# Selecting each expert's top 80 tokens by ranks instead of by MAX8 rounds, in a sparse attention and expert kernel

## The chip, the cores and the metric

The kernel runs on one NeuronCore of a Trainium2 chip. The metric is the device time of one execution in microseconds (us). Five engines work side by side: TensorE (PE, with its weight loads shown apart as PEld), VectorE (DVE), ScalarE (ACT), GpSimd (POOL) and SyncE (SP, which here only issues DMAs). They meet only through semaphores.

## The reference, cut to what matters

```
# attention: B=4 batches, H=8 heads, S=768 tokens, D=64; keys in chunks of 32
ub     = sum(max(q*kmin, q*kmax))          # bound of each chunk's score
top    = 6 chunks of the largest ub, causal
attn   = softmax(scale * q@k.T, masked to those chunks and to earlier keys)
x      = (attn @ v), as rows (B*S, H*D) = (3072, 512)
# experts: E=8, capacity 80
logits = x @ w_gate ; expert = argmax ; gate = max of softmax(logits)
for e in range(E):
    tok = tokens of expert e ; if more than 80: the 80 with the largest gate
    out[tok] = gate[tok] * (relu(x[tok] @ w1[e]) @ w2[e])      # all other rows 0
```

## The kernel before, in words

The attention loop has 16 steps `i`, one for each pair of heads; four pairs make a batch (`b = i // 4`, pair 0 to 3 of it). In a step, `scores` (L489) computes six blocks of transposed scores on TensorE, half of each in turn in the PSUM tiles SC0 and SC1, and ScalarE takes the exponentials into EXB (key E0 to E5). `folds` (L514) masks the diagonal blocks on GpSimd and adds the blocks up into ES, from which `sums` (L545) on TensorE makes the softmax denominators. `values` (L531) multiplies by v into OB, ScalarE copies that to oT. The sums, the row transposes (`rows`, L562) and the scaling of pair `i - 1` stand inside the step of pair `i`, so that GpSimd has a step's time for its additions. `bounds`, `transposes`, `unselT` prepare later pairs. `scale_rows` (L567) writes the rows `x` to DRAM (x_rows) by a DMA of SyncE, and the pair's share of the logits to lgp.

The order on every engine is the order in which this code is written: the helper `op` (L72) puts each instruction at the end of its engine's queue and adds the semaphore waits for the tiles it reads and writes.

When a batch has all its pairs, the next batch's pair 0 makes its gates: `gate_in` and `gate` (VectorE: row maxima, argmax, gate value), `gate_digits` (VectorE: the token's number and its gate in three bf16 parts, per expert, in RC), and `gate_T` (L603: six transposes into SC0 and one ScalarE copy to `cand`, 8 rows, one for each expert). Then `rounds` spreads ten rounds over the batch's pairs: MAX8 finds the eight largest of a row of 848 (768 new tokens and the 80 kept), MATCH_REPLACE8 takes them out.

After the loop comes the tail. The last pair's sums, rows, scaling and the last batch's gate run one behind the other; ten more rounds on rows of 768 (L724), a merge with the 80 kept ones, the threshold of each expert (L729), masks, two matmuls and a scan that number the chosen tokens (L738 to L753), one-hot rows (L759) and 24 matmuls (L764) give `idx`, the 80 token numbers of each expert. Eight indirect DMAs of GpSimd gather these rows (L781), and eight experts run: `turn`, `up`, `down` and an indirect DMA of the result (L821). The experts' weights come by DMAs of GpSimd's queue during the loop (`wload`, two or one in a step); w2 of the last expert takes the place of E0 and E1 in EXB after the loop. Eight memsets on GpSimd in the tail (L723) clear the gathers' destinations. `warm` issues matmuls whose result nobody reads; 40 of them stand ahead of the first pair.

## Time and profile before

| | us |
|---|---|
| median of 3 runs | 349.25 (348.21 to 350.11) |
| the profiled execution: its own time | 347.47 |
| its span, first to last instruction | 345.7 |
| busy in the span: PE, PEld, DVE, ACT, POOL | 288.7, 183.4, 232.9, 149.3, 231.2 |

The span leaves out 1.77 us around the instructions. Busy times are of one execution and overlap; what they say of the end depends on who waits for whom, which the chain of waits and the timelines show. A PE record counts twice for an f32 matmul: eight f32 matmuls show as x16.

### The profile page before, as it was taken

The numbers are of one execution on the slowest core, as the hardware profiler recorded it, in microseconds if no ns is written. First come the engines' busy times: TensorE is split into PE (matmuls) and PEld (weight loads), VectorE is DVE, ScalarE is ACT, GpSimd is POOL, SyncE is SP. The second block draws the span as 40 slices with busy tenths as digits, with TensorE's granted clock in tenths as the row PEclk, the third lists the DMA queues.
The fourth block names the chain that finished last, engine by engine and source line by source line (L and its number), as shares of the span: only waits on it lengthen the run. The fifth ranks groups of instructions, "written<-read, shape, count | busy, mean of one in ns | idle before, by whom it ended". The sixth has DMA issues, their size and how long they took to land.

```text
span 345.7 us, 7895 instructions
## 1 busy us (share of the span) xinstructions
PE 288.7 (83%) x3244; PEld 183.4 (53%) x3244; DVE 232.9 (67%) x591; ACT 149.3 (43%) x202; POOL 231.2 (67%) x313
## 2 busy tenths in 40 slices
PE   7499999999989999998999999899999210126993
PEld 6356656575646566565656565656556100025771
DVE  3815435262988797979697887979797489871441
ACT  3265645555554646555555546554545000002320
POOL 5059888787868797786878787869798900007322
PEclk9789999999999999999999999999999955556999
DMA  9946879899758999798999779864907450001121
GB/s 175 193 91 139 150 145 184 240 225 165 160 101 184 266 196 189 151 161 258 183 179 191 140 151 255 144 108 87 163 11 138 58 86 1 0 2 55 53 59 57
DMA packets 104964, 47.50 MB, mean 137 GB/s; under 512 B 88955, under 2 KB 97269, under 8 KB 104928
## 3 DMA queue, kind: packets, MB, share of 16 engines
q1 hardware_dynamic: 89920, 27.94, 34.6%
q0 software_dynamic: 13440, 18.67, 33.1%
q10 hardware_dynamic: 1568, 0.39, 0.6%
q8 instruction: 25, 0.41, 0.5%
q14 instruction: 11, 0.09, 0.1%
HBM read 53.10 MB, written 10.75 MB: 185 GB/s over the span
## 4 chain that ended last, share of the span: by engine, by line
PE 73%; issue 12%; ACT 6%; POOL 4%; DVE 3%; DMA 1%; POOLq 0%; DVEq 0%
PE SC L498 23%; PE OB L539 20%; PE SC L425 6%; PE SC L504 5%; ACT EXB L509 5%; PE OB L815 4%; PE OB L564 3%; PE M L554 3%; PE SC L800 3%; PE M L549 2%; POOL ES L528 2%; PE MB L485 2%; DMA kn<-x_rows,idx 1%; ACT cand L607 1%; ACT unsT L487 1%
## 5 line engine op out<-in xcount | busy, mean ns | idle before, releaser
L528 POOL TENSOR_TENSOR ES<-ES,EXB 128x256 f32<-128x256 f32 (+1 forms) x112 | 106.1, 960 | 6.4
L509 ACT ACTIVATE EXB<-SC 128x1024 f32<-128x1024 f32 x96 | 86.3, 917 | 52.1 <-PE SC L504 50.4
L498 PE MATMUL SC<-qT,kT 64*128 64x512 f32 (+3 forms) x512 | 98.7, 473 | 2.8 <-ACT cand L607 2.7
L539 PE MATMUL OB<-EXB,vn 128*64 128x256 f32 (+2 forms) x704 | 71.9, 360 | 0.0
L539 PEld LDWEIGHTS OB<-EXB,vn 128*64 128x64 f32 x704 | 46.7, 137 | 23.0 <-issue 8.8
L498 PEld LDWEIGHTS SC<-qT,kT 64*128 64x128 f32 x512 | 42.4, 189 | 26.5 <-issue 15.5
L528 POOL TENSOR_TENSOR ES<-EXB 128x768 f32<-128x768 f32 (+1 forms) x32 | 49.3, 1542 | 1.3
L626 DVE MAX8 top<-cand 8x8 f32<-8x848 f32 (+1 forms) x40 | 40.3, 1008 | 2.2 <-ACT cand L607 1.3
L519 POOL TENSOR_SCALAR_AFFINE_SELECT EXB<-EXB 128x256 f32<-128x256 f32 x80 | 31.6, 406 | 12.1 <-ACT EXB L509 12.1
L504 PE MATMUL SC<-unsT,ind 64*128 64x384 bf16 (+3 forms) x256 | 39.0, 298 | 0.0
L543 ACT ACTIVATE oT<-OB 128x512 f32<-128x512 f32 (+1 forms) x32 | 15.7, 491 | 52.7 <-PE OB L539 52.7
L628 DVE MATCH_REPLACE8 cand<-top,cand 8x848 f32<-8x848 f32 (+1 forms) x36 | 35.7, 992 | 0.0
L572 DVE TENSOR_TENSOR xp<-OB,rden 128x768 bf16<-128x768 f32 x16 | 15.3, 958 | 24.4 <-PE OB L564 24.3
L781 POOL DMA_INDIRECT qn<-x_rows,idx x4 | 3.9, 980 | 35.0 <-issue 35.0
L504 PEld LDWEIGHTS SC<-unsT,ind 64*128 64x128 bf16 x256 | 13.0, 95 | 18.6 <-issue 8.5
L557 DVE STREAM_TRANSPOSE M<-M 128x192 f32<-128x192 f32 x16 | 6.2, 384 | 24.3 <-PE M L554 24.3
L467 DVE STREAM_TRANSPOSE M<-M 128x160 f32<-128x160 f32 x16 | 5.8, 366 | 21.5 <-PE MB L463 21.1
L430 ACT ACTIVATE qT<-SC 128x768 f32<-128x768 f32 x16 | 13.0, 812 | 14.7 <-PE SC L425 14.7
L792 ACT ACTIVATE rq<-MB 128x320 bf16<-128x320 bf16 x4 | 1.7, 437 | 39.3 <-PE MB L789 39.3
L519 POOL TENSOR_SCALAR_AFFINE_SELECT ES<-EXB 128x256 f32<-128x256 f32 x16 | 6.5, 404 | 17.6 <-PE M L554 16.3
L732 PE MATMUL M<-dg,ones 8*128 8x8 f32 x2 | 0.6, 367 | 20.9 <-DVE dg L730 20.9
L821 POOL DMA_INDIRECT out_dram<-EXB,idx x8 | 7.4, 920 | 14.6 <-DVE EXB L819 14.6
(141 smaller groups left out, 449.3 us busy)
## 6 DMA issues: line engine op xcount, KB each, us to landing
w1s<-in_moe_w_dram POOLq DMA_DIRECT2D x8, 1024.0 KB, 8.4
w2s<-in_moe_w_dram POOLq DMA_DIRECT2D x7, 1024.0 KB, 10.2
qn<-in_q_dram SPq DMA_DIRECT2D x32, 192.0 KB, 4.0
vn<-in_v_dram SPq DMA_DIRECT2D x32, 192.0 KB, 2.9
out_dram<-w1s SPq DMA_DIRECT2D x4, 1536.0 KB, 7.6
kn<-in_k_dram SPq DMA_DIRECT2D x30, 192.0 KB, 3.7
x_rows<-xp SPq DMA_DIRECT2D x16, 192.0 KB, 4.5
EXB<-in_moe_w_dram POOLq DMA_DIRECT2D x1, 1024.0 KB, 9.7
```

The costliest lines, as they stand in the source:

```text
L425: op("pe", lambda: pe.transpose(SC[ps][:, ts(t)], a, ident_f[:]), r=[f"{nm}{s}0", f"{nm}{s}1", "ident_f"], w=[f"SC{ps}"], inc=(t == NT - 1))
L498: op("pe", lambda: pe.matmul(o, kT[j][pr, ts(kt)], qT[j][pr, q0:q1], start=True, stop=False), r=[f"kT{j}", f"qT{j}"], w=[f"SC{s}"], inc=False)
L504: op("pe", lambda: pe.matmul(o, ind[pr, ts(kt)], unsT[j][pr, b0 - 128:q1 - 128], start=False, stop=True), r=[f"ind{h}", f"unsT{j}"], w=[f" ...
L509: op("act", lambda: ac.activation(Ex(st, None, 0, W), src, ACTF.Exp, scale=SCALE), r=[f"SC{s}"], w=[f"E{st}"])
L519: op("gp", lambda: gp.affine_select(ad, a, pattern=[[0, 2], [1, 128]], compare_op=ALU.is_ge, fill=0.0, base=0, channel_multiplier=-1), r=[ ...
L528: op("gp", lambda: gp.tensor_tensor(o, in0, in1, ALU.add), r=[f"E{s2}", f"E{first[0]}"] if first else [f"E{s2}"] + kt, w=kt)
L539: op("pe", lambda: pe.matmul(OB[pr, q0:q1], vn[s][:, kt, h, :], ex, start=(n == 0), stop=last), r=[f"vn{s}{h}", "ES0" if st is None else f ...
L543: op("act", lambda: ac.activation(oT[:, q0:q1], OB[:, q0:q1], ACTF.Copy), r=[f"O{bk}"], w=[f"oT{bk}"])
L572: op("dve", lambda: ve.tensor_tensor(xo, xi, rx, ALU.mult), r=["O0", "O1", "rden"], w=["xp"])
L626: op("dve", lambda: ve.max(dst, cv), r=["cand"], w=[f"top{int(last)}{n}"])
L628: op("dve", lambda: ve.match_replace(cv, dst, cv, -2.0), r=["cand", f"top{int(last)}{n}"], w=["cand"])
L815: op("pe", lambda: pe.matmul(o, hTv(e)[:, fb * CAP:(fb + 1) * CAP], w2v(e)[:, fb, :], start=(fb == 0), stop=(fb == FB - 1)), r=[f"hT{s}{fb ...
```

## The change

The rounds go, and the ranks of the tokens are counted. `rank_row` transposes the six columns of gates, each spread over 128 columns, and ScalarE copies the result to G: every partition holds the 768 gates of the batch in its row, and `rank_pred` puts a copy, a hair smaller, beside it (it settles ties by position). `rank_cmp` compares, for one tile of 128 tokens, 640 of the row's gates with the tile's own gate on each partition; `rank_own` and `rank_diag` do the same for the 128 tokens of the tile itself. `rank_count` multiplies these 0/1 tiles by the tokens' one-hot expert rows on TensorE (44 matmuls with 32 columns of weights): each token gets its rank among those of its expert. `rank_slot` turns ranks into one-hot rows of 80 slots, `table` multiplies them by RC, and `merge` takes, slot by slot, the larger of the 80 kept and of the 80 new in opposite order. `sort_rows`, `sort_rank` and `sort_apply` bring the 80 kept back into order after the second and third batch. For the batches 0 to 2 this is spread over pairs 0, 1 and 2 of the next batch; for the last one it is in the tail. The compare results of batches 0 to 2 lie in the weight tiles of the last two experts, whose loads move to the steps 14 and later.

The last pair's folds of block 5 are left out; `sums_last` sums their pieces with 72 matmuls instead. The pair's logits are scaled ahead of its rows. `clear_xg` clears the gathers' destinations on VectorE in steps 14 and 15. Three groups of dummy matmuls (56, 16, 44) stand in the tail.

```diff
                         if lo:
-                            folds(st)
+                            folds(i, st)
...
-                        for (s2, c2, q0, q1) in ADDS[st]:
+                        for (s2, c2, q0, q1) in ADDS[st] if st < 5 or i < NP - 1 else []:
...
+                def sums_last(i):
+                    pieces = [(None, 0, 0, 512), (2, 256, 512, 768)] + ADDS[5]
+                    for n, (st, c0, q0, q1) in enumerate(pieces):
+                        for h in range(2):
+                            for c in range(4):
...
+                                op("pe", lambda: pe.matmul(M0[c * 32:c * 32 + 32, q0 // 4:q1 // 4], onc[:, h, :], a,
+                                                           start=(n == 0 and h == 0), stop=False),
...
+                    sums_lg(i, False, True)
+                    sums_out()
...
-                def gate_T(b):
-                    for t in range(NT):
-                        op("pe", lambda: pe.transpose(SC[0][0:E, ts(t)], gv[:, b * NT + t, :], ident_f[:]),
...
-                    op("act", lambda: ac.activation(cand[:, CAP:CAP + S], SC[0][0:E, 0:S], ACTF.Copy), r=["SC0"], w=["cand"])
...
-                def top_round(n, last):
...
+                PRED = 1.0 - 2.0 ** -24
+
+                def rank_row(b):
+                    for t in range(NT):
+                        gb = bass.AP(gt6, t, [[NT, 128], [0, 128]])
+                        op("pe", lambda: pe.transpose(SC[1][:, ts(t)], gb, ident_f[:]),
+                           r=["gt6", "ident_f"], w=["SC1"], inc=(t == NT - 1))
+                    op("act", lambda: ac.activation(G[:, S:2 * S], SC[1][:, 0:S], ACTF.Copy), r=["SC1"], w=["grow"])
+
+                def rank_pred():
+                    op("act", lambda: ac.activation(G[:, 0:S], G[:, S:2 * S], ACTF.Copy, scale=PRED), r=["grow"], w=["growP"])
+
+                def rank_own(b):
+                    e, q = ("gp", gp) if b == B - 1 else ("dve", ve)
...
+                    op(e, lambda: q.tensor_tensor(T1v(b).rearrange("p (a b) -> p a b", a=NT), tq, gb, ALU.mult),
...
+                def rank_diag(b):
...
+                        op("dve", lambda: ve.tensor_tensor(o, a, g, ALU.is_ge), r=["T1", "grow"] + Ck(b, NT - 1),
...
+                def rank_cmp(b, *jts):
+                    for jt in jts:
+                        gj = gt6[:, jt:jt + 1]
+                        o = Cs(b, jt, 1, 128, S - 128)[:, 0, :]
+                        if b < B - 1:
+                            o = o.rearrange("p (a b) -> p a b", a=NT - 1)
+                        op("dve", lambda: ve.tensor_scalar(o, G[:, (jt + 1) * 128:(jt + 1) * 128 + S - 128], gj, None, ALU.is_lt),
...
+                def rank_count(b):
...
+                                op("pe", lambda: pe.matmul(MBf[c * 32:c * 32 + 32, o * 32:(o + hi - lo) * 32], ohb[:, jt, :], Cv[:, :, c, :],
...
+                def rank_slot(b):
+                    op("dve", lambda: ve.transpose(MBf[:, 192:384], MBf[:, 0:192]), r=["MB"], w=["cnT"])
...
+                    op("dve", lambda: ve.tensor_tensor(OHS[:].rearrange("p (a b) -> p a b", a=NT), io, rb, ALU.is_equal),
...
+                def table(b):
+                    for t in range(NT):
+                        op("pe", lambda: pe.matmul(M0[0:CAP, 0:5 * E], OHS[:, t * CAP:(t + 1) * CAP],
...
+                def merge(b):
...
+                    gsum(gN[:], tv, ["M0"], "gN")
+                    op("dve", lambda: ve.tensor_tensor(mk[:], gN[:], gT[:], ALU.is_gt), r=["gN", "gT"], w=["mk"])
...
+                    op("dve", lambda: ve.copy_predicated(dT[:, 0:nd, :], mb, tv[:, 0:nd, :]), r=["mk", "M0", "dT"], w=["dT"])
...
+                def sort_rows(split):
+                    for e in range(E):
...
+                        op("pe", lambda: pe.transpose(o, gb, ident_f[0:CAP, 0:CAP]),
...
+                def sort_rank():
...
+                    op("dve", lambda: ve.tensor_tensor(SA, SA, gb, ALU.is_ge), r=["grow", "gT"], w=["grow"])
+                    op("dve", lambda: ve.tensor_reduce(rk8[:], SA, AX, ALU.add), r=["grow"], w=["rk8"])
...
+                def sort_apply():
+                    for e in range(E):
+                        op("pe", lambda: pe.matmul(MBf[0:CAP, e * 5:(e + 1) * 5], SP[:, e, :], dTb[:, :, e], start=True, stop=True),
...
                 for i in range(NP):
+                    kk, bb = i % NPB, i // NPB - 1
+                    live = bb >= 0
                     scores(i, 0, 2)
                     if i:
                         sums(i - 1)
-                    folds(0, 1)
+                    folds(i, 0, 1)
+                    if live and kk == 1:
+                        rank_pred()
+                        rank_cmp(bb, 5)
+                    if live and kk == 2:
+                        rank_cmp(bb, 1, 0)
                     scores(i, 2, 4)
                     if i:
                         rows(i - 1)
                         scale_rows(i - 1)
+                        scale_lg(i - 1)
+                    if live and kk == 2:
+                        rank_count(bb)
+                        rank_slot(bb)
+                    if i == 12:
+                        sort_apply()
+                    if i == NP - 1:
+                        sort_rows(True)
+                        clear_xg(1)
                     scores(i, 4, 6)
...
+                    if live and kk == 0:
+                        gate_digits(bb)
+                        gate_cols(bb)
+                        rank_own(bb)
+                    if live and kk == 1:
+                        rank_diag(bb)
+                        rank_cmp(bb, 4, 3, 2)
+                    if i == NP - 1:
+                        sort_rank()
                     values(i)
...
-                    if first:
-                        gate_T(i // NPB - 1)
-                    rounds(i, 1)
-                    if i < NP - 1:
+                    if live and kk == 0:
+                        rank_row(bb)
+                    if live and kk == 2:
+                        table(bb)
+                        merge(bb)
+                    if i == 11:
+                        sort_rows(False)
+                        sort_rank()
+                    if i == NP - 2:
+                        clear_xg(0)
+                        wload(E - 2, 1)
+                        wload(E - 1, 0)
+                    elif i < NP - 3:
                         wload(i // 2, i % 2)
-                    rounds(i, 2)
...
                 b = B - 1
-                sums(NP - 1)
+                sort_apply()
+                sums_last(NP - 1)
+                scale_lg(NP - 1)
                 rows(NP - 1)
+                gate_in(b)
+                wload(E - 1, 1)
+                gate(b)
+                rank_row(b)
+                rank_pred()
+                rank_own(b)
+                warm(56)
                 scale_rows(NP - 1)
-                gate_in(b)
-                gate(b)
-                gate_T(b)
                 gate_digits(b)
-                wload(E - 1, 1)
...
-                for n in range(ROUNDS):
-                    top_round(n, True)
...
-                op("dve", lambda: ve.tensor_tensor_scan(scn, keep[:], OB[:, 512:512 + NW], 0.0, ALU.mult, ALU.add),
...
+                rank_cmp(b, 5)
+                rank_diag(b)
+                rank_cmp(b, *ORDER[1:])
+                rank_count(b)
+                warm(16)
+                gate_cols(b)
+                rank_slot(b)
+                table(b)
+                warm(44)
+                merge(b)
```

Three places show the new order. First TensorE at the end of the loop: the last products with v (OB<-EXB,vn), the late sums (L549, L554 before), the rows, the last batch's gate. Before:

```order
L539 MATMUL OB<-EXB,vn 64x128
L549 MATMUL M_22<-oT,wg 32x192 [waits sy_dve,sy_act]
L549 MATMUL M_22<-oT,wg 32x192 x3
L554 MATMUL M_22<-ES,onc 32x192 [waits sy_gp]
L554 MATMUL M_22<-ES,onc 32x192 x7
L564 MATMUL OB<-ident_f,oT 128x128 x6
L605 MATMUL SC_19<-ident_f,gv 8x128 [waits sy_dve]
L605 MATMUL SC_19<-ident_f,gv 8x128 x5
```

and after the change, with the sums as L583 and L557:

```order
L761 MATMUL MB<-dTb,G 80x5 x7
L583 MATMUL M_21<-ES,onc 32x128 x8
L583 MATMUL M_21<-EXB,onc 32x64 x24
L583 MATMUL M_21<-EXB,onc 32x32 x16
L583 MATMUL M_21<-EXB,onc 32x64 x8
L583 MATMUL M_21<-EXB,onc 32x32 x16
L557 MATMUL M_21<-oT,wg 32x192 [waits sy_act]
L557 MATMUL M_21<-oT,wg 32x192 x3
L592 MATMUL OB<-ident_f,oT 128x128 x6
L649 MATMUL SC_19<-ident_f,gt_50 128x128 [waits sy_dve]
L649 MATMUL SC_19<-ident_f,gt_50 128x128 x5
L768 MATMUL SC_18<-ident_bf 128x128 x56
```

The sums' wait for GpSimd (sy_gp) is gone and the matmuls have become many and short; 56 dummy matmuls stand behind the gate's transposes.

Second VectorE in the tail, from the last round to the last one-hot rows. Before:

```order
L626 MAX top<-cand 8x8 [waits sy_dve]
L727 SCALAR_TENSOR_TENSOR top<-top 8x80 [waits sy_dve]
L729 TENSOR_REDUCE thr_70<-top 8x1 [waits sy_dve]
L730 TENSOR_SCALAR dg_71<-ident_f,thr_70 8x8 [waits sy_dve]
L738 TENSOR_TENSOR kT<-gv,M_22 128x192 [waits sy_pe]
L739 TENSOR_TENSOR kT<-gv,M_22 128x192
L744 SCALAR_TENSOR_TENSOR oT<-kT,OB 128x384 [waits sy_pe,sy_gp]
L746 TENSOR_TENSOR oT<-oT,OB 128x384 [waits sy_dve]
L747 TENSOR_TENSOR oT<-oT,OB 128x384 [waits sy_pe,sy_dve]
```

and after the change, where L677 are the compares, L668 the tiles' own, L639 and L641 the columns RC and the rest `rank_slot`:

```order
L677 TENSOR_SCALAR EXB<-G,gt_50 128x640 [waits sy_gp,sy_act]
L668 TENSOR_TENSOR EXB<-EXB,G 128x6x128 [waits sy_dve]
L677 TENSOR_SCALAR EXB<-G,gt_50 128x640 [waits sy_dve,sy_act]
L677 TENSOR_SCALAR EXB<-G,gt_50 128x640 [waits sy_dve] x4
L639 TENSOR_TENSOR RC<-ohb,idc 128x6x16
L641 TENSOR_TENSOR RC<-ohb,gsp 128x6x24
L695 STREAM_TRANSPOSE MB<-MB 128x192 [waits sy_pe]
L697 TENSOR_TENSOR cn_70<-MB,ohb 128x48 [waits sy_dve]
L698 TENSOR_REDUCE rk_71<-cn_70 128x6 [waits sy_dve]
L701 TENSOR_TENSOR OHS<-iota_67,rk_71 128x480 [waits sy_dve]
```

The ten rounds, the threshold, the masks and the scan have given way to six compares, one for the tiles' own tokens, and one set of one-hot rows.

Third TensorE in the last pair, between its rows and its fifth block of scores. Before:

```order
L504 MATMUL SC_20<-unsT,ind 128x256 x2
L564 MATMUL OB<-ident_f,oT 128x128 x6
L498 MATMUL SC_19<-qT,kT 128x384 [waits sy_act]
L498 MATMUL SC_19<-qT,kT 128x384
L504 MATMUL SC_19<-unsT,ind 128x384 x2
```

and after the change, where L739 is `sort_rows` and M_21 the PSUM tile that VectorE reads the logits from:

```order
L592 MATMUL OB<-ident_f,oT 128x128 x6
L739 MATMUL M_21<-ident_f,gT 80x80 [waits sy_dve]
L739 MATMUL M_21<-ident_f,gT 80x80 x5
L739 MATMUL MB<-ident_f,gT 80x80 x2
L507 MATMUL SC_18<-qT,kT 128x384 [waits sy_act]
L507 MATMUL SC_18<-qT,kT 128x384
```

Eight transposes now stand there with a wait for VectorE.

## Rows read from the trace of the kernel before

**Rows 1.** The chain that ended last, whole run: start us, us, what.
```profile
223.83 0.76 ACT cand L607
224.63 1.13 PE SC L498 x4
...
240.37 1.06 PE SC L498 x4
...
243.13 0.65 PE M L554 x16
```

**Rows 2.** The same chain, asked from 254 to 275 us.
```profile
253.95 0.39 PE MB L485 x5
...
260.33 0.81 PE OB L564 x6
...
270.53 0.73 POOL ES L528
...
271.31 0.90 PE M L554 x16
```

**Rows 3.** Timeline, 262 to 346 us: start us, us, engine, line, shapes [idle before <-releaser].
```profile
267.52 0.38 ACT L543 ACTIVATE oT<-OB 128x256 f32<-128x256 f32 x1 [1.78 <-PE OB L539]
...
272.23 0.40 DVE L557 STREAM_TRANSPOSE M<-M 128x192 f32<-128x192 f32 x1 [4.39 <-PE M L554]
...
273.19 0.96 DVE L572 TENSOR_TENSOR xp<-OB,rden 128x768 bf16<-128x768 f32 x1
...
274.06 0.32 DVE L576 TENSOR_TENSOR lgp<-M,rden 128x96 f32<-128x96 f32 x1
...
276.49 0.19 DVE L599 RECIPROCAL gt<-lsum 128x6 f32<-128x6 f32 x1
...
279.29 0.95 DVE L626 MAX8 top<-cand 8x8 f32<-8x768 f32 x1 [1.29 <-ACT cand L607]
...
309.44 0.16 DVE L771 SCALAR_TENSOR_TENSOR idx<-idz,idt 80x8 uint32<-80x8 f32 x1
...
310.54 1.05 POOL L781 DMA_INDIRECT qn<-x_rows,idx  x1 [34.12 <-issue]
```

**Rows 4.** Stretches: A:B us, busy by engine, granted clock, DMA share, GB/s.
```profile
274.00:276.00 2.00, 0.00 (x0) 0.00 (x0) 1.83 (x9) 0.24 (x1) 2.00 (x6) 1.00 1.06 153
276.00:278.00 2.00, 1.02 (x6) 0.62 (x6) 1.83 (x11) 0.00 (x0) 0.43 (x1) 0.57 1.16 167
```

**Rows 5.** The chain, whole run, in the expert stage.
```profile
314.86 2.13 PE SC L800 x32
317.26 1.21 PE SC L800 x32
```

**Rows 6.** Groups by shape: line engine op, shapes xcount | busy us, mean ns | idle before.
```profile
L528 POOL TENSOR_TENSOR ES<-EXB 128x768 f32<-128x768 f32 x16 | 29.0, 1811 | 1.3
...
L439 DVE TENSOR_REDUCE kmm<-kT 128x24 f32<-128x768 f32 x16 | 15.2, 953 | 0.5
...
L759 DVE TENSOR_TENSOR ES<-iota,sl 128x480 bf16<-128x480 f32 x4 | 2.4, 654 | 0.0
```

**Rows 7.** The page's DMA issues: issue xcount, KB each, median us to landing.
```profile
x_rows<-xp SPq DMA_DIRECT2D x16, 192.0 KB, 4.5
```

**Rows 8.** Timeline of TensorE, 205 to 228 us.
```profile
222.93 0.82 PE L605 MATMUL SC<-ident_f,gv 128*8 128x128 f32 x6
```

**Rows 9.** Timeline of VectorE, one line in the loop and in the tail.
```profile
218.55 1.30 DVE L593 SCALAR_TENSOR_TENSOR oh<-lg,rank_c 128x48 f32<-128x48 f32 x1
...
275.48 0.21 DVE L593 SCALAR_TENSOR_TENSOR oh<-lg,rank_c 128x48 f32<-128x48 f32 x1
```

**Rows 10.** Waits: engine, line <- releaser: us in total, times, longest.
```profile
POOL ES L519 <- PE M L554: 16.3, 12, 1.6
```

**Rows 11.** Timeline, the last pair, 262 to 263 us.
```profile
262.05 0.32 DVE L576 TENSOR_TENSOR lgp<-M,rden 128x96 f32<-128x96 f32 x1
...
262.68 0.44 PE L539 MATMUL OB<-ES,vn 128*64 128x128 f32 x4
```

More of the change, by code (lines that the diff above doesn't have):

```diff
@@ L543, in values, with sums_lg @@
                         op("act", lambda: ac.activation(oT[:, q0:q1], OB[:, q0:q1], ACTF.Copy), r=[f"O{bk}"], w=[f"oT{bk}"])
-                def sums(i):
+                def sums_lg(i, start, stop):
                     p = i % NPB
@@ L549, in sums, with sums_out @@
                         op("pe", lambda: pe.matmul(M0[c * 32:c * 32 + 32, 0:192], wg[:, p, :], stripes(oT, c * 32, 0, 0, None),
-                                                   start=True, stop=False),
-                           r=["oT0", "oT1", "wg"] + WG, w=["M0"], inc=False)
+                                                   start=start, stop=stop),
+                           r=["oT0", "oT1", "wg"] + WG, w=["M0"], inc=(stop and c == 3))
+                def sums_out():
+                    op("dve", lambda: ve.transpose(M0[:, 192:384], M0[:, 0:192]), r=["M0"], w=["rows_s"])
+                    op("dve", lambda: ve.tensor_scalar(rden[:], rows_s[:, :, 16:18], 1e-9, None, ALU.add),
+                       r=["rows_s", "M0"], w=["rden"])
+                    op("dve", lambda: ve.reciprocal(rden[:], rden[:]), r=["rden"], w=["rden"])
+                def sums(i):
+                    sums_lg(i, True, False)
                     for h in range(2):
@@ new lines, in _body @@
+                ORDER = [5, 4, 3, 2, 1, 0]
+                def rank_count(b):
+                    for n, jt in enumerate(ORDER):
+                        for lo, hi, o in ((0, NT - jt, jt), (NT - jt, NT, 0)):
+                            if lo == hi:
+                                continue
+                            Cv = Cs(b, jt, 1, lo * 128, (hi - lo) * 128)[:, 0, :].rearrange("p (t c i) -> p t c i", c=4, i=32)
+                            last = jt == ORDER[-1]
+                            for c in range(4):
+                                op("pe", lambda: pe.matmul(MBf[c * 32:c * 32 + 32, o * 32:(o + hi - lo) * 32], ohb[:, jt, :], Cv[:, :, c, :],
+                                                           start=(n == 0 and lo == 0), stop=last),
+                                   r=["ohb", f"C{jt}", f"D{jt}"] + Ck(b, jt), w=["MB"], inc=(last and c == 3))
@@ L687, in _body @@
                         load(i + 4, "qk")
-                    rounds(i, 0)
+                    if live and kk == 0:
+                        gate_digits(bb)
[6 more added lines that the diff above has]
+                        sort_rank()
                     values(i)
```

251 lines of the change are left out of this document (124 added, 127 removed).

## The prediction

> **What bounds the kernel now.** I read the chain that ended last first. In the loop it stays on TensorE: a pair's first scores to the next pair's are 240.37 - 224.63 = 15.74 us [rows 1], and what stands between is matmuls with short hand-overs. VectorE's rounds lie beside that and end nothing there. What an edit adds to TensorE's queue in the loop is therefore paid, and what it takes from VectorE there is not.
>
> At the end of the loop the chain leaves TensorE. GpSimd's last folds end at 270.53 + 0.73 = 271.26, and the last pair's sums (L554) start at 271.31 [rows 2], though the products with v were over when ScalarE took them at 267.52 [rows 3]. From there the timeline of the tail is one line: sums, gate, rounds from 279.29 on, masks and numbering, idx at 309.44 + 0.16 = 309.60, first gather at 310.54 [rows 3]. From 267.52 to 310.54 are 43.0 us in which TensorE does next to nothing; its granted clock is 1.00 (2.4 GHz) until 276 and averages 0.57 over the next two us, on its way to 1.2 GHz [rows 4]. The first expert then pays for the low level: its first 32 matmuls take 2.13 us on the chain, the next expert's 1.21 [rows 5].
>
> The change has thus three prices: a shorter tail, a longer loop, a warmer start of the experts.
>
> **The tail, step by step**, t counted from 267.52, when the products with v are done (all later numbers in us).
>
> Eight small matmuls of sort_apply, at 0.39 / 5 = 0.08 each as the bf16 transposes [rows 2]: 0.6. The late sums: 72 f32 matmuls, 144 records, 4096 columns in all. Eight with 192 columns each, 1536 in all, take 0.65 in the loop [rows 1]. By columns that makes 0.65 x 4096 / 1536 = 1.7, by records 144 x 0.65 / 16 = 5.9. I take 2.7: those in the loop are long ones, four column groups side by side, where the columns count; most of the new ones have 64. Four matmuls for the logits, half of eight: 0.4. So t = 3.7.
>
> Gate: from L557 at 272.23 to the gate value at 276.49 + 0.19 = 276.68 are 4.45; the rows' scaling goes behind it and takes its 274.06 - 273.19 = 0.87 along [rows 3]. 3.6 remain: t = 7.3.
>
> Two lines follow side by side. TensorE transposes six tiles (0.81, as L564 [rows 2]), ScalarE copies them (0.76, as L607 [rows 1]): the row G is there at 8.9, its second copy at 9.7. VectorE has the one-hot compare (0.2), the scaling (0.96 [rows 3]) and four short digit steps (0.2 each, as L599): 9.3. GpSimd's product for the tiles' own tokens takes 1.81 [rows 6], until 9.1, and may hold VectorE's short steps a little. I start the compares at 9.6.
>
> A compare of 640 columns has no row. From above: 953 ns for 768 columns of one f32 input in SBUF [rows 6], so 0.79. From below: 0.19, what an instruction with six columns costs [rows 3]. I take the middle, 0.5: six are 3.0, the 768-wide own compare 0.96 and a hand-over 0.1: t = 13.7. The Trainium skill (VectorE: DVE Perf Modes, The perf-mode tier table) lets a tensor_scalar on f32 in SBUF run at two columns a cycle and a tensor_tensor at one; no row of before shows a long one; its estimate is 0.39 a compare and a sum 0.7 shorter.
>
> TensorE's counting runs along; its last eight matmuls come after the last compare: 0.4, with the columns RC beside them on VectorE. rank_slot: transpose 0.40 [rows 3], two short steps, one-hot rows 0.65 [rows 6], hand-overs: 1.6. Table: six matmuls and hand-overs 0.6. merge up to idx: four short steps 0.95. From idx to the gather 310.54 - 309.60 = 0.94, as before [rows 3]. Sum: 18.2. The tail shrinks by 43.0 - 18.2 = 24.8.
>
> Two covers. The 56 dummy matmuls start at about 8.1 and last 56 x 0.08 = 4.5 at the full clock, over before the compares end at 13.7; at the low clock, by the ratio 2.13 / 1.21 = 1.76 of [rows 5], the six transposes and the dummies end at 16.6 and the count is late (rival 1). And the gathers also wait for the last x_rows write, issued at about 8.6; with a median of 4.5 to landing [rows 7] it lands at 13.1, four us ahead of idx.
>
> **The loop.** Per batch TensorE gains 44 counting matmuls. Singly, at 0.08, they would take 3.5, in four column groups a quarter, 0.9; at the 0.041 per record of the sums they take 1.8. I take 1.1. Six table matmuls are 0.5. The six transposes stay, but go to SC1: before, the next pair's first scores waited for ScalarE's copy out of SC0, from 222.93 + 0.81 (transposes) to 224.63, which are 0.9 [rows 1, 8]; now they use the other half and that wait goes. What is late next is the copy of kT, which also reads SC1 and stands behind the gate on VectorE; it moves ahead of the digits. So 0.7 a batch, 2.1 for three. Sorting in steps 11 and 12 adds eight transposes (0.7) and sort_apply (0.6). Together 3.4, with 0 (all of it in gaps) to 9 (below) as bounds.
>
> VectorE loses six us of rounds a pair and gets about as much in the busiest one; its work lies ahead of the sums and behind the next keys as before. Here one thing speaks against the change: GpSimd. The same instruction (L593, two inputs in SBUF) takes 1.30 in the loop, with GpSimd adding, and 0.21 in the tail [rows 9]. Many of the new VectorE steps have two inputs in SBUF. GpSimd's own room is its wait for the sums, 12 times, 16.3 in all, 1.36 each [rows 10]. I cost the holds at nothing, since own, diagonal, one-hot rows and short steps are about 3.4 a batch and the room of three pairs is 4.1.
> The Trainium skill (SBUF — State Buffer, SBUF: two separate sides) says that VectorE and GpSimd share a port pair as an exclusive lock, held for a whole instruction. Rows 9 agree for VectorE as the one that waits; no row shows GpSimd waiting.
>
> **The last pair.** The eight sort transposes write the PSUM tile that VectorE reads for the logits until 262.05 + 0.32 = 262.37 [rows 11]. TensorE was through its rows at 260.33 + 0.81 = 261.14 [rows 2] and went on to the last two blocks, 1.54, up to the first product with v at 262.68 [rows 11]. Now it waits until 262.4, transposes 0.7, and the products start at 264.7: 2.0 later. At least 0.7 (the transposes alone), at most 2.8 (ScalarE's two copies then hold the next exponential too).
>
> **The experts** start warm if the dummies keep the clock: 2.13 - 1.21 = 0.9 less.
>
> **The sum.** -24.8 + 3.4 + 2.0 - 0.9 = -20.3. The profiled execution took 347.47 (a span of 345.7 and 1.77 around it); it becomes 327.2. The median is 349.25, 1.78 above that execution; carried over, the forecast is 328.9.
>
> **Rivals.**
> 1. TensorE becomes the tail's bound. The late sums go by records (5.9 instead of 2.7: 3.2 more), and the clock is low after the gate, so that the count ends at 16.6 + 1.8 = 18.4 instead of 14.1: 4.3 more. 328.9 + 7.5 = 336.4. For it: the clock fell in this very stretch before. Against: TensorE is now busy until the gate's last 3 us, and the clock was still 1.00 after the 3.8 us between the products and the sums [rows 3, 4], which held four short matmuls only.
> 2. Holds between VectorE and GpSimd. If the compares hold it as well (6 x 0.79 = 4.7), a batch holds 8.2, three 24.6, the sorting four steps of 0.8: 27.8. Less the room of 16.3, 11.5 are paid: 340.4. For it: rows 9. Against: no slower GpSimd instruction is seen, and one-input steps are not known to hold.
> 3. Slower. The same holds, with no room: they fall where TensorE waits for masked blocks or for the sums, and all 27.8 land on it: 356.7, 7.4 above before. It decides from 20.3 of the 27.8 on. For it: the chain is on TensorE with no gaps. Against: 12 waits with room are counted [rows 10], and only two pairs in four hold much.
> 4. The change does not shorten the end: the gathers wait for something else until 310. Only the x_rows write could be that, and 4.5 to landing speaks against it. About 349.
>
> **Chances.** Forecast 0.75; its own range is 322 (compares 1.9 less, sums 1.0, loop 3.4, last pair 1.3, all at their low ends, 321.3, rounded in) to 333. Rival 1 0.12, rival 2 0.08, rival 3 0.03, rival 4 0.02. The range goes to rival 1: 322 to 337. Under 0.5% is what a measurement of this kernel can hardly tell from no change. Faster: 0.75 + 0.12 + 0.08 = 0.95; same 0.02; slower 0.03.
>
> **What would show it.** Right: no wait of L571 or the late sums for GpSimd at the end; 16 to 20 us from the last product with v to the first gather; compares in the tail well under 0.8 us; granted clock 1.00 from there into the experts, whose first 32 matmuls take about 1.2; pairs of batches 1 to 3 that are longer by about 0.7 a batch. Wrong: the count (L690) behind the dummies (L768) instead of behind the compares; GpSimd's additions longer or later in pairs 1 and 2 of a batch, and TensorE waiting for them; a gather that waits for x_rows; a last pair that is not longer.

## The result, and the profile after

The changed kernel takes 329.5 us, the median of four runs (328.5 to 331.0), against 349.7 (348.2 to 350.5) in the same comparison: a ratio of 0.943, 95% interval 0.938 to 0.948. The forecast was 328.9 with a range of 322 to 337. The profiled execution took 329.96 with a span of 328.2, against 347.47 and 345.7.

The stages of the two spans, cut at the same events (first scores of pair 0, products with v of the last pair, ScalarE's last oT copy, first gather):

| stage | before | after | difference | forecast |
|---|---|---|---|---|
| start to the first scores | 16.27 | 17.17 | +0.9 | 0 |
| fifteen pairs | | | +1.35 | +3.4 |
| last pair, up to its products with v | | | +1.8 | +2.0 |
| tail, oT copy to first gather | 43.0 | 19.7 | -23.3 | -24.8 |
| experts, first gather to the end | 35.2 | 36.9 | +1.75 | -0.9 |
| span | 345.7 | 328.2 | -17.5 | -20.3 |

So the total hit, but not because each term did: the start, the tail and the experts came out worse than forecast, the loop better, the last pair nearly as forecast. On the spans the gain is 2.8 short. The medians hide that, because the profiled execution of before was 2.2 below its median and that of after 0.4 above: this part of the hit is luck.

The tail on TensorE in the timeline of the changed kernel (start, busy us, engine, line, operation, out<-in, shapes, records; in brackets the idle time before and what ended it):

```profile
271.85 0.64 PE L583 MATMUL M<-ES,onc 128*32 128x128 f32 x16
272.31 1.49 PE L583 MATMUL M<-EXB,onc 128*32 128x64 f32 x110
275.58 0.35 PE L583 MATMUL M<-EXB,onc 128*32 128x32 f32 x18 [1.79 <-issue]
275.74 0.52 PE L557 MATMUL M<-oT,wg 128*32 128x192 f32 x8
276.19 0.87 PE L592 MATMUL OB<-ident_f,oT 128*128 128x128 f32 x6
279.69 1.54 PE L649 MATMUL SC<-ident_f,gt 128*128 128x128 f32 x6 [2.62 <-DVE gt L628]
281.02 4.89 PE L768 MATMUL SC<-ident_bf 128*128 128x128 bf16 x56
286.73 0.71 PE L690 MATMUL MB<-EXB,ohb 128*32 128x32 bf16 x44 [0.82 <-DVE EXB L677]
287.37 1.07 PE L768 MATMUL SC<-ident_bf 128*128 128x128 bf16 x16
289.11 0.41 PE L709 MATMUL M<-RC,OHS 128*80 128x40 bf16 x6 [0.68 <-DVE OHS L701]
289.36 2.62 PE L768 MATMUL SC<-ident_bf 128*128 128x128 bf16 x44
294.04 0.32 PE L904 MATMUL MB<-ident_bf,qn 80*128 80x80 bf16 x4 [2.06 <-DMA qn<-x_rows,idx]
295.47 0.45 PE L904 MATMUL M<-ident_bf,kn 80*128 80x80 bf16 x4 [1.11 <-DMA kn<-x_rows,idx]
295.71 2.33 PE L915 MATMUL SC<-rq,w1s 128*128 128x80 bf16 x32
```

From the start of the sums to the first gather there were 39.2 us [rows 2, 3]; now there are 19.4. The wait for GpSimd's folds [rows 2] is gone. Two things are not as forecast: a gap of 1.79 inside the late sums that no semaphore ended, and all 44 counting matmuls behind the last compare. VectorE's compares in the same timeline, and the first gather on GpSimd:

```profile
282.11 0.55 DVE L677 TENSOR_SCALAR EXB<-G,gt 128x640 bf16<-128x640 f32 x1 [0.27 <-ACT G L651]
282.69 0.96 DVE L668 TENSOR_TENSOR EXB<-EXB,G 128x768 bf16<-128x768 f32 x1
283.76 2.91 DVE L677 TENSOR_SCALAR EXB<-G,gt 128x640 bf16<-128x640 f32 x5
290.17 0.16 DVE L725 SCALAR_TENSOR_TENSOR idx<-dT 80x8 uint32<-80x8 f32 x1
291.29 1.08 POOL L896 DMA_INDIRECT qn<-x_rows,idx  x1 [10.10 <-DVE gT L729]
```

The granted clock, by stretches of the span (the last three figures of a row are the granted clock, DMA share and GB/s):

```profile
276.00:280.00 4.00, 1.38 (x16) 0.95 (x9) 3.34 (x14) 0.24 (x1) 1.19 (x2) 0.69 0.35 42
280.00:284.00 4.00, 4.00 (x34) 3.94 (x33) 3.48 (x8) 1.66 (x2) 1.19 (x1) 0.50 1.18 177
288.00:292.00 4.00, 3.31 (x58) 2.95 (x55) 1.74 (x8) 0.00 (x0) 0.71 (x1) 1.00 0.00 0
292.00:296.00 4.00, 0.85 (x13) 0.72 (x14) 0.00 (x0) 0.49 (x2) 3.08 (x4) 0.82 0.18 54
296.00:300.00 4.00, 4.00 (x64) 4.00 (x62) 0.49 (x1) 1.70 (x4) 3.05 (x4) 0.50 0.24 65
```

Before, the clock left 2.4 GHz at 276 and was back only behind the first expert's 32 matmuls [rows 4, 5]. Now the clock is at 1.2 GHz during the gate's stretch, comes back under the dummies, and falls a second time when TensorE has waited for the gathers: the first two experts run at 1.2 GHz, 2.33 busy for their 32 matmuls against 1.31 from the third expert on.

In the loop, the costs that the forecast put on TensorE came and went within a batch. GpSimd's waits (what waited, for what, total us, times, longest) and the compares by shape (busy us, mean ns):

```profile
POOL ES L528 <- PE M L571: 21.1, 14, 2.2
```
```profile
L677 DVE TENSOR_SCALAR w1s<-G,gt 128x640 bf16<-128x640 f32 x15 | 14.3, 954 | 0.4
L677 DVE TENSOR_SCALAR EXB<-G,gt 128x640 bf16<-128x640 f32 x6 | 3.3, 554 | 0.5 <-ACT G L651 0.3
```

GpSimd's room for folds is not used up: 21.1 us where it was 16.3 [rows 10].

### The profile page after: what moved, and what is told of

Read it like the earlier page. It is cut to its first block, busy times and chain, and to the rows that moved or that the text cites. A ratio compares the mean times of both kernels' runs of the same rounds, so it can differ in the third digit from the quotient of the medians.

```text
span 328.2 us, 8726 instructions
## 1 busy us (share of the span) xinstructions
PE 301.4 (92%) x3692; PEld 197.3 (60%) x3692; DVE 187.4 (57%) x539; ACT 153.6 (47%) x209; POOL 227.3 (69%) x297
## 4 chain that ended last, share of the span: by engine, by line
PE 81%; DVE 7%; ACT 5%; issue 3%; POOL 2%; DMA 1%; POOLq 0%; DVEq 0%
PE SC L507 24%; PE OB L548 23%; PE SC L434 6%; PE SC L513 5%; ACT EXB L518 5%; PE OB L930 4%; PE OB L592 3%; PE SC L915 3%; PE M L571 3%; PE M L557 2%; PE MB L494 2%; PE SC L649 1%; DVE EXB L677 1%; PE MB L690 1%; DMA kn<-x_rows,idx 1%
## 5 line engine op out<-in xcount | busy, mean ns | idle before, releaser
L537 POOL TENSOR_TENSOR ES<-ES,EXB 128x256 f32<-128x256 f32 (+1 forms) x106 | 102.8, 982 | 6.0
L528 POOL TENSOR_SCALAR_AFFINE_SELECT EXB<-EXB 128x256 f32<-128x256 f32 x80 | 32.3, 414 | 14.3 <-ACT EXB L518 14.3
L513 PE MATMUL SC<-unsT,ind 64*128 64x384 bf16 (+3 forms) x256 | 39.2, 299 | 0.0
L528 POOL TENSOR_SCALAR_AFFINE_SELECT ES<-EXB 128x256 f32<-128x256 f32 x16 | 6.9, 433 | 22.3 <-PE M L571 21.1
L434 PE MATMUL SC<-ident_f,qn 128*128 128x128 f32 x96 | 13.7, 279 | 4.0 <-ACT EXB L518 2.0
L448 DVE TENSOR_REDUCE kmm<-kT 128x24 f32<-128x768 f32 x16 | 15.2, 953 | 0.5
L434 PEld LDWEIGHTS SC<-ident_f,qn 128*128 128x128 f32 x96 | 10.2, 141 | 8.6 <-issue 5.8
L446 DVE COPY kT<-SC 128x768 f32<-128x768 f32 x16 | 15.1, 947 | 0.0
L449 DVE TENSOR_REDUCE kmx<-kT 128x24 f32<-128x768 f32 x16 | 15.1, 943 | 0.0
```

The source lines that it names most:

```text
L434: op("pe", lambda: pe.transpose(SC[ps][:, ts(t)], a, ident_f[:]), r=[f"{nm}{s}0", f"{nm}{s}1", "ident_f"], w=[f"SC{ps}"], inc=(t == NT - 1))
L446: op("dve", lambda: ve.tensor_copy(kT[j][:], SC[1][:, 0:S]), r=["SC1"], w=[f"kT{j}"])
L448: op("dve", lambda: ve.tensor_reduce(kmm[j][:, 0, 0:NCH], kv, AX, ALU.min), r=[f"kT{j}"], w=[f"kmm{j}"])
L449: op("dve", lambda: ve.tensor_reduce(kmx[:], kv, AX, ALU.max), r=[f"kT{j}"], w=["kmx"])
L513: op("pe", lambda: pe.matmul(o, ind[pr, ts(kt)], unsT[j][pr, b0 - 128:q1 - 128], start=False, stop=True), r=[f"ind{h}", f"unsT{j}"], w=[f" ...
L528: op("gp", lambda: gp.affine_select(ad, a, pattern=[[0, 2], [1, 128]], compare_op=ALU.is_ge, fill=0.0, base=0, channel_multiplier=-1), r=[ ...
```

## Experiments

Each ratio is to the kernel before on the same chip; the changed kernel's is 0.943. The four edits from "No dummies" to "The folds back" ran where the kernel before took 349.1. All others ran on two slower chips (353.6 and 353.9), so the changed kernel was run again on the first of these two; ratios and stages are compared, not times.

**The changed kernel again.** No edit.

> The changed kernel, unaltered, on the same chip as the last three, to see what varies between two executions of the same code. Theory A (whether the granted clock falls between the dummies and the first expert is a matter of some tenths of a us, as the kernel with the folds back kept 1.00 there with the same dummies and the same gaps): the stage from the first gather to the end takes 34.2 to 36.9, and the first pair's scores start at 16.6 to 17.2. Theory B (both belong to this code): 36.9 and 17.2 again.

Ratio 0.9457 (0.9439 to 0.9475). The first scores come at 17.16 and the tail takes 19.36, as before; the experts take 41.85. The second expert on TensorE, by the timeline:

```profile
297.61 0.84 PE L915 MATMUL SC<-rq,w1s 128*128 128x80 bf16 x14
298.69 0.20 PE L915 MATMUL SC<-rq,w1s 128*128 128x80 bf16 x1 [0.24 <-issue]
299.41 0.32 PE L915 MATMUL SC<-rq,w1s 128*128 128x80 bf16 x4 [0.52 <-issue]
300.82 0.30 PE L915 MATMUL SC<-rq,w1s 128*128 128x80 bf16 x4 [1.10 <-issue]
301.55 0.23 PE L915 MATMUL SC<-rq,w1s 128*128 128x80 bf16 x1 [0.42 <-issue]
302.26 0.71 PE L915 MATMUL SC<-rq,w1s 128*128 128x80 bf16 x8 [0.49 <-issue]
```

These pauses, which nothing in the profile ends, stand in every kernel run on the two slower chips and in none of the other runs. For the experts neither theory's number holds there; the start is that of theory B. That the kernel before has these pauses too would explain its 353.6 against 349.1, but no trace of it on these chips was taken.

**No dummies in the tail.**
```diff
-                warm(56)
-                warm(16)
-                warm(44)
```


> The 116 dummy matmuls of the tail are left out; everything else as in the changed kernel. Theory A (the dummies lift the clock in the tail, and only a part of that comes back): without them the granted clock stays at 0.50 from the gate to the first experts; the count (0.71) and rank_slot's and table's TensorE steps take up to twice as long, about 0.8 us more on the path, and the first expert is as slow as it is with them (2.13 for its first 32 matmuls): 0.5 to 1.2 us slower than the changed kernel. Theory B (the dummies delay real work, since they stand ahead of the count in TensorE's queue): same or up to 0.5 us faster. Theory C (the dummies decide the gain of the experts): 2 us slower or more.

Ratio 0.9462 (0.9417 to 0.9507), by the ratios 1.0 us slower, within the intervals. The clock stays at 0.50 from 276 to 299.9, the count takes 1.15 and the tail 21.0, 1.3 more (0.7 of it a longer gap in the sums, which stand ahead of these dummies); the experts take 35.9, 1.0 less. That is theory A in the trace: what the dummies win in the tail they lose again, because the clock falls anew behind them. The times alone don't separate it from theory B.

**Dummies up to the gathers.**
```diff
-                warm(44)
+                warm(82)
                 turn(0)
+                warm(18)
                     turn(e + 1)
+                    if e == 0:
+                        warm(14)
```


> The last 44 dummies become 82, and 18 and 14 more stand between the first expert's transposes and the second's and behind these, so that TensorE is never idle for long until the first expert's matmuls. Theory A (the clock falls at 294.8 because TensorE waits for the gather from 291.98 to 294.04 and again to 295.47): the granted clock stays at 1.00 into the experts, the first two groups of 32 matmuls take about 1.2 instead of 2.13 and the first down half: 2.0 to 3.0 us faster than the changed kernel. Theory B (the clock falls anyway at this point, whatever TensorE does): same, or up to 0.5 us slower for dummies in the way.

Ratio 0.938 (0.9335 to 0.9425). The experts take 34.75, 2.2 less than in the changed kernel; the clock is 1.00 and the first two experts are fast:

```profile
295.28 1.31 PE L915 MATMUL SC<-rq,w1s 128*128 128x80 bf16 x32
296.57 1.31 PE L915 MATMUL SC<-rq,w1s 128*128 128x80 bf16 x32
```

Theory A holds. The intervals overlap; the trace decides.

**Sort transposes behind the last blocks.**
```diff
+                    scores(i, 4, 6)
                     if i == NP - 1:
                         sort_rows(True)
                         clear_xg(1)
-                    scores(i, 4, 6)
```


> In the last pair the eight sort transposes go behind the last two blocks of scores instead of ahead of them. Theory A (the 1.82 us that the last pair has gained are TensorE waiting 1.29 us for VectorE's logits and the transposes' 0.6 behind it): the wait goes, the transposes stay, 1.0 to 1.4 us faster. Theory B (the sorting's row copies on ScalarE or its four steps on VectorE become the bound, which end at 269.2): the products with v or sort_apply wait for them, and no more than 0.3 us are gained.

Ratio 0.9375 (0.933 to 0.9421). The wait for VectorE's logits (1.29) is gone:

```profile
265.18 0.61 PE L739 MATMUL M<-ident_f,gT 80*80 80x80 f32 x6
```

The last pair, from its first scores to its products with v, takes 8.87 instead of 10.23: 1.36, within A's range. In the span the products start only 0.9 earlier, at 265.86 instead of 266.75, because the first pair of this execution happened to be 0.47 longer; over the runs that leave the first pair as it is it takes 15.2 to 16.3, while every other pair repeats to 0.02. So a stage is compared by its own length, not by where it starts. Sort_rank's last step now ends at 270.33, 0.2 ahead of sort_apply at 270.55: B is near.

**The folds back on GpSimd.**
```diff
-  for (s2, c2, q0, q1) in ADDS[st] if st < 5 or i < NP - 1 else []:
+  for (s2, c2, q0, q1) in ADDS[st]:
-                sums_last(NP - 1)
+                sums(NP - 1)
```


> The last pair's late sums are undone: GpSimd adds the last block's seven pieces again, and TensorE sums the folded rows in eight column matmuls as in the loop. Theory A (the late sums are worth the chain over GpSimd less their own 3.6 us): GpSimd's additions end about 3.7 us after the products with v, the sums take 0.9 instead of 3.6 and come to the gate about 1.0 us later than in the changed kernel: 0.5 to 1.5 us slower. Theory B (without the gap of 1.79 us the late sums are worth more, and so the folds cost all that): 2.5 us slower or more. Theory C (GpSimd is free earlier in this kernel, and the late sums bring nothing): same or faster.

Ratio 0.9448 (0.9393 to 0.9503). GpSimd adds until 275.2, and the sums start behind it:

```profile
275.29 1.51 PE L571 MATMUL M<-ES,onc 128*32 128x192 f32 x16 [3.26 <-POOL ES L537]
```

The tail takes 20.8, 1.1 more: A by the trace, though the ratio alone can't be told from the changed kernel's 0.943. Part of the 1.1 is the clock, which fell to 0.50 ahead of these sums: they take 1.51 and the rows behind them 1.54, instead of some 0.9 each. The late sums, the most elaborate part, bring one microsecond as written. This run shows something else as well: same dummies, same waits for the gathers (2.06 and 1.13), and here the clock did not fall. Its experts take 34.16, 1.0 less than before the change:

```profile
296.18 1.31 PE L915 MATMUL SC<-rq,w1s 128*128 128x80 bf16 x32
297.47 1.31 PE L915 MATMUL SC<-rq,w1s 128*128 128x80 bf16 x32
```

**Weights later.**
```diff
-                        wload(E - 2, 1)
-                        wload(E - 1, 0)
+                wload(E - 2, 1)
+                wload(E - 1, 0)
                 wload(E - 1, 1)
```


> The two loads of expert weights that the last but one pair issues (2 MB, they fill the DMA engines from 261 to 273 us) are issued in the tail, beside the third one. Theory A (the gap of 1.79 us in the late sums is TensorE waiting for a piece of its code, whose packet of 0.02 MB comes at 273.2 behind these loads): the packet comes earlier and the gap goes or shrinks below 0.6; the late sums end about 1.5 us earlier, and the kernel is 1 to 1.5 us faster unless the later loads collide with the gathers. Theory B (the gap is the rate at which short instructions can be delivered, whatever the DMA engines carry): the gap stays at 1.5 to 2 us. Theory C (a wait on a semaphore that the profile does not show): the gap stays as well, and it moves with the last piece in e6.

Ratio 0.9448 (0.9408 to 0.9489). The gap is 2.12 long, but the edit did not bring the case that theory A speaks of: GpSimd had nothing left to do and issued the two loads at 268.1 and 269.0, so the DMA engines were full when the packet came at 273.1, as in the changed kernel (share 1.13 and 1.10 in the microsecond before). The run decides between none of the three.

**GpSimd adds two pieces.**
```diff
- pieces = [(None, 0, 0, 512), (2, 256, 512, 768)] + ADDS[5]
+ pieces = [(None, 0, 0, S)] + ADDS[5][2:]
  # last pair, step 4: GpSimd also runs ADDS[5][:2]
```


> GpSimd adds the two pieces of block 3 in the last pair, in its idle time before the last select, and the late sums are 48 matmuls instead of 72 (192 columns wide in the first eight). Theory A (the gap belongs to a long run of short instructions, or to a place in the code that 48 matmuls don't reach before the gate): no gap in the sums, which take about 1.6 in all instead of 3.6: 1.5 to 2 us faster. Theory B (the gap stands before the last piece whatever comes before, a wait on E5): it stays at about 1.8 or grows, and the kernel is at most 0.4 us faster.

Ratio 0.9358 (0.9315 to 0.9401), the tail 17.3 instead of 19.7; 0.4 of these 2.4 go back to the last products with v, which end later, behind GpSimd's last select. No gap:

```profile
272.31 0.86 PE L583 MATMUL M<-ES,onc 128*32 128x192 f32 x16
272.99 0.94 PE L583 MATMUL M<-EXB,onc 128*32 128x32 f32 x78
```

Theory A; a wait on E5 would have stayed. Two additions in a stretch in which GpSimd was idle are worth more than all the late sums were.

**Twelve dummies less at the start.**
```diff
-                warm(40)
+                warm(28)
```


> The 40 dummies at the very start become 28, so that everything behind them stands 12 matmuls earlier in TensorE's code. Theory A (the gap in the late sums is TensorE at the end of a block of its code, waiting for the next one: in seven runs it ended 2.3 to 2.5 us after a packet of the instruction queue): the gap moves back by those 12 one-pass matmuls, to behind some 130 to 150 of the 144 records, or out of the sums. Theory B (it is a matter of how many short instructions follow each other): it stays behind record 126. The time may change by up to 0.5 us at the start, by the clock.

Ratio 0.9417 (0.9397 to 0.9437). The gap moves from record 126 to record 138, by exactly those twelve:

```profile
270.96 1.58 PE L583 MATMUL M<-EXB,onc 128*32 128x64 f32 x122
274.05 0.23 PE L583 MATMUL M<-EXB,onc 128*32 128x32 f32 x3 [1.51 <-issue]
```

And in each run with the gap one packet of the instruction queue falls just ahead of it; here in 271 to 272 (packets, MB, share):

```profile
q8 instruction: 1, 0.02, 5.5%
```

Theory A: the gap goes with the place in the code, and TensorE goes on 2.3 to 2.5 us after the packet's start in all ten runs with a gap. The reading that fits them all is that TensorE is at the end of what it has of its code; 138 records pass in 2.0 us at this place, faster than the next piece comes. The view does not name the engine that a packet is for, so that it is TensorE's is inferred.

**Setup later.**
```diff
+                    if i == 0:
+                        setup_late()   # triQ, triS, ohb, idc
                     values(i)
```


> The setup of triQ, triS, ohb and the token numbers (nine VectorE steps and three of GpSimd) goes from ahead of the first kT copy to behind the first pair's scores. Theory A (the 1.07 us that the first scores start later come from these steps on VectorE ahead of the kT copy, 0.36, and from the bounds matmuls that fall behind the drop of the granted clock, 0.5): the first scores start at 16.3 again, 0.7 to 1.1 us faster. Theory B (the start is bound by the loads, and the rest is a matter of chance in the clock): within 0.3 us of the changed kernel.

Ratio 0.9353 (0.931 to 0.940). The first scores start at 14.58 instead of 17.17, 2.6 earlier, more than A said: the kT copy starts at 7.87 instead of 9.66, since the token numbers' steps and their waits for GpSimd, which the kernel before has too, leave that path with the new ones; and the bounds matmuls and the beginning of the first scores still have the clock at 1.00. (The expectation counts nine VectorE steps; the edit moves seven, and the three of GpSimd.)

```profile
14.58 1.64 PE L498 MATMUL SC<-qT,kT 64*128 64x512 f32 x4
```

**Flat compares in the loop.**
```diff
-                        if b < B - 1:
-                            o = o.rearrange("p (a b) -> p a b", a=NT - 1)
```


> In the loop the compare writes its 640 columns as one row, as it does in the tail, not as five rows of 128. Theory A (one-input compares in the loop are stretched by GpSimd's additions, up to 2.0 us, since they have to wait for the port, and the written form makes no difference): same, within 0.5 us, compares in the loop 0.5 to 2 us as now. Theory B (the flat form takes the port from GpSimd and holds it off, the five-row form doesn't): GpSimd's additions beside the compares get longer, the compares shorter, and TensorE waits more for folded rows: 1 us slower or more.

Ratio 0.9447 (0.9406 to 0.9488). Compares in the loop take 0.48 to 1.99 (the 15 that write to w1s take 0.93 on average, 0.95 in the changed kernel), GpSimd's additions keep their mean of 0.98: theory A, as far as the written form goes.

**Dummies through the gate, counting by tile.**
```diff
                 rows(NP - 1)
+                warm(44)
-                warm(56)
+                warm(84)
- r=["ohb", f"C{jt}", f"D{jt}"] + Ck(b, jt)
+ r=["ohb", f"C{jt}", f"D{jt}"] + (Ck(b, jt) if b < B - 1 else [])
```


> 44 dummies more behind the last pair's row transposes, so that TensorE is busy during the gate, 84 instead of 56 behind the gate's rows, and the count's matmuls of the last batch wait for their own compare only. Theory A (the clock falls because TensorE is idle during the gate, and the count stands behind all compares only because their output shares its names): granted clock 1.00 from the loop on, the six transposes of the gate values take 0.85 instead of 1.54, the count ends 0.15 behind the last compare instead of 0.8: 1.0 to 1.6 us faster. Theory B (the dummies come in the way of the gate's transposes or the count): same or slower. In this chip's loop and experts nothing changes under either.

Ratio 0.9387 (0.9371 to 0.9403) beside 0.9457 of the changed kernel on that chip: 2.5 us. The tail is 0.7 shorter (18.7), less than A's 1.0 to 1.6; the rest is the loop's 0.5, all of it in the first pair, and the experts' 1.6; this edit explains neither. Theory A in its mechanism:

```profile
278.62 0.87 PE L649 MATMUL SC<-ident_f,gt 128*128 128x128 f32 x6 [0.17 <-DVE gt L628]
279.33 4.85 PE L768 MATMUL SC<-ident_bf 128*128 128x128 bf16 x84
284.11 0.86 PE L690 MATMUL MB<-EXB,ohb 128*32 128x32 bf16 x40
285.29 0.27 PE L690 MATMUL MB<-EXB,ohb 128*32 128x192 bf16 x4 [0.32 <-DVE EXB L677]
```

The last four counting matmuls alone wait for the last compare. The clock fell again at the gathers.

**All together.** The edits of the five runs that helped (without the bridge's 14).

> All that helped together: setup behind the first pair's scores, sort transposes behind the last blocks, GpSimd adding two of the last pieces, dummies through the gate and up to the gathers (without the last 14 of the bridge), count by its own compares. If the parts add (2.6 start, 0.9 last pair, 2.4 sums, 2 to 3 experts, 1 to 1.5 tail): 8 to 10 us faster than the changed kernel, a ratio of 0.913 to 0.922 to the kernel before. If the clock's low stretch only moves to another place, or the gap of the code comes up elsewhere: 5 to 7.

Ratio 0.9354 (0.9331 to 0.9376), 3.5 us ahead of the changed kernel on the same chip, not 8 to 10, nor 5 to 7. Against the changed kernel's span there the start is 2.5 shorter, the loop 1.6, the tail 1.8; the experts are 1.6 longer. Two parts get in each other's way: GpSimd's two additions lie beside two sort steps of VectorE, which take 1.44 and 1.78 instead of 0.82, and sort_apply waits 1.00 for them.

```profile
263.39 1.44 DVE L743 TENSOR_TENSOR G<-G,triS 80x640 f32<-80x640 f32 x1 [0.67 <-ACT G L735]
264.87 1.78 DVE L744 TENSOR_TENSOR G<-G,gT 80x640 f32<-80x640 f32 x1
```

And the pauses come earlier, 5.6 us of them:

```profile
288.91 0.32 PE L909 MATMUL MB<-ident_bf,qn 80*128 80x80 bf16 x4 [1.10 <-issue]
290.67 0.24 PE L909 MATMUL M<-ident_bf,kn 80*128 80x80 bf16 x2 [0.37 <-issue]
294.04 1.37 PE L920 MATMUL SC<-rq,w1s 128*128 128x80 bf16 x16 [3.13 <-issue]
296.37 1.23 PE L920 MATMUL SC<-rq,w1s 128*128 128x80 bf16 x16 [0.96 <-issue]
```

The bridge is spent on them: the clock falls in the pause ahead of the first expert. On a chip without pauses the sum may be larger; it was not run there. What the pauses are stays open. The place in the code it is not: with 72 dummies more ahead of it the second expert paused behind its 15th matmul, without them behind the 14th. Counted from the first gather, though, the times repeat. In all eight runs on the slower chips the last pause ends 11.3 to 11.4 us behind the first gather, with all edits too, where the pauses begin 2.8 us behind it instead of 7.5, at the first transposes. In the other seven one ends at 8.4 to 8.5 and another at 9.8 to 9.9. That points at the gathers, but no run shows what TensorE waits for.

## Why the prediction held, term by term

**The experts: the step that failed.** "The experts start warm if the dummies keep the clock: 2.13 - 1.21 = 0.9 less." The price was right, 1.0 in the run with the folds back. The condition was not worked out: the forecast ended the dummies behind the table and left TensorE idle from idx to the gathers' data, 2.06 and 1.11 us. In the profiled execution the clock fell there, and two experts and the first down half paid: +1.75 instead of -0.9, 2.65 off. Whether it falls there varies: with the folds back it did not. Dummies up to the data take it back.

**The tail: right mechanism, 1.5 long.** Sums and logits ended at t = 4.7 instead of 3.7. The matmuls themselves were faster than costed (2.9 without the gap). The gap added 1.8, a cost that no term had; by the run with twelve dummies less it is the arrival of the code. The sign "granted clock 1.00 from there into the experts" failed: the clock fell at 277.5 already, the six transposes of the gates took 1.54 instead of 0.81, and the first compare waited 0.27 for their copy.

The compares took 0.58 each with their gaps, within the bounds of 0.19 and 0.79. With GpSimd idle a compare took 0.55, in the loop 0.48 at the least, against 0.79 for one column at a time by rows 6. By the Trainium skill (VectorE: DVE Perf Modes, The perf-mode tier table) 2048 f32 columns take 1227 ns in a tensor_scalar and 2293 in a tensor_tensor; brought down to 640 columns at that rate, a compare has an estimated 0.49, not the forecast's 0.39, and the trace agrees in the loop and is 0.06 longer in the tail.

The count was costed at 0.4 for its last eight matmuls and took 0.8 for all 44: the compares' output shares four names, and each matmul waited for the last writer of them. That stood in the code, in the list Ck of the names that a compare writes. Rival 1's "count behind the dummies" did not come: these began at the low clock and ended at 285.9, 0.8 ahead of the last compare; its other half, sums by records, did not either. The rest, rank_slot to gather, took 3.8 instead of 4.1. Of the 23.3 the late sums are some 1.1 and the dummies 1.3 at most, by the runs without them; the rest is the selection and the order around it, by subtraction, since no run put the rounds alone back.

**The loop: +1.35 instead of +3.4.** The wait that rank_row's move to SC1 removes gave 0.96, as forecast (pair 0 of the second and third batch takes 16.32 instead of 17.28). The count and the table cost 1.07 a batch instead of 1.6, the sorting 0.85 instead of 1.3. Per batch that leaves 0.1, not 0.7: the 44 counting matmuls take 0.9, and of the table little is left on the path. The other 0.17 lie in the first pair, which varies by more than that.

**The start: +0.9, not forecast.** Five new setup steps on VectorE, in the place of four old ones, were costed nowhere. The first kT copy starts 0.36 later (9.66 instead of 9.30), and the bounds then run at the lower clock. In other executions of the same code the first scores came at 16.6 to 17.2, so about half of it varies.

**The last pair: +1.8 for +2.0**, by the wait that was named:

```profile
264.46 0.61 PE L739 MATMUL M<-ident_f,gT 80*80 80x80 f32 x6 [1.29 <-DVE lgp L600]
```

**Rivals 2 and 3** named a price that exists, but most of it fell on the other engine: beside GpSimd's additions the compares took up to 1.99, and the same sort steps up to 1.78. GpSimd waited too, so one of the named signs of being wrong came. Where a compare began first, its addition of 768 columns took 1.98 to 1.99 instead of 1.81, in pairs 1 and 2 of the last three batches:

```profile
100.51 0.48 DVE L677 TENSOR_SCALAR w2s<-G,gt 128x640 bf16<-128x640 f32 x1
100.68 1.99 POOL L537 TENSOR_TENSOR ES<-EXB 128x768 f32<-128x768 f32 x1
```

Shape by shape the additions got some 3 us longer in the whole run, not 27.8, and this came out of GpSimd's room, which grew; TensorE waited for the additions no longer than before ahead of its products with v (2.5 us both times). The Trainium skill (SBUF — State Buffer, SBUF: two separate sides) speaks of an exclusive lock, which whoever starts first holds for the whole instruction. The trace agrees in that either engine waits behind the other.

The errors cancel in part: start +0.9, loop -2.05, tail +1.5, experts +2.65, last pair -0.2 make 2.8. That the forecast of 328.9 still lies within 0.7 of the median is due to the two profiled executions, 2.2 under and 0.4 above their medians.

## What to carry to other kernels

Dummy matmuls that lift the clock pay only if they reach the work that needs it: count the idle time up to the data, not up to the last instruction. A long run of short matmuls has a price that no busy time shows, the arrival of its code; moving two additions to an idle engine removed it. Parts that were measured alone are added only after looking which engine each now runs beside.

## What the runs showed of the hardware

- TensorE stopped 1.4 to 2.5 us in the middle of 144 short records, always at the same place of its code, and went on 2.3 to 2.5 us after an instruction packet of 0.02 MB. With twelve dummies less at the program's start the place moved by twelve records.
- On the two slower chips TensorE paused in the first experts, 0.2 to 3.1 us at a time between groups of one to sixteen matmuls, the last time until 11.3 to 11.4 us behind the first gather in all eight runs; nothing in the profile ends these pauses. The experts took 40.3 to 43.5 there, and 34.2 to 36.9 where it never did.
- With the same dummies and nearly the same idle time behind them the granted clock fell before or in the first experts in nine profiled executions and stayed at 1.00 in one (waits of 2.06 and 1.13; 2.06 and 1.11 in the changed kernel, where it fell).
- A compare of 640 f32 columns with one input takes 0.48 to 0.55 us where it doesn't stand behind an addition of GpSimd's and up to 2.0 where it does; an addition of 768 columns that a compare is ahead of takes 1.99 instead of 1.81.
